# An attention and state-space kernel on one core: first loads as tasks of the list, lag 0 reordered by GpSimd, and a new order of all tasks

## The chip, the core and the metric

The kernel runs on one core of a Trainium2 chip. TensorE (PE) multiplies matrices, VectorE (DVE) and ScalarE (ACT) do elementwise work, GpSimd (POOL) copies, fills and starts transfers, and SyncE (SP) starts transfers. The metric is the device time of one execution in microseconds (us).

## The reference

Two branches read the same x (2048 positions, 640 channels) and are mixed by a gate per position. Branch a is attention over 8 positions at distances 0, 2, ... 14, with 32 heads of 20 channels. Branch b is a long convolution of x with a kernel K that is generated from 192 complex states per channel.

```
g = sigmoid((x * gate_w).sum(-1, keepdims=True))
qkv = x @ wqkv                                   # 640 -> 3 * 640
logits = q . k at 8 dilated positions, masked, * 20**-0.5
a = (softmax(logits) . v) @ wo
dt = exp(log_dt)
P = exp(dt * (A_re + i A_im) * l)                # 640 x 192 x 2048
K = Re(sum over n of C * P * dt * B)             # 640 x 2048
y = irfft(rfft(u padded) * rfft(K padded))[:L] + u * Dskip
out = g * a + (1 - g) * y
```

## The kernel before, in words

The whole program is a list of 1384 tasks (`SEQ`, L50). A number names a task, a letter behind it the engine that runs it where there is a choice: A ScalarE, D VectorE, S SyncE's queue, G GpSimd's queue. `Plan.emit` (L132) writes the tasks in that order and chains the instructions of each engine, so each engine runs its tasks strictly in the order of the list, and a task that waits holds up all that stand behind it on that engine.

The work has these parts.

- **Parameters** (`SSMParams.build`, L530). Six tiles of 128x960 (real and imaginary parts of A, B, C) become twelve bfloat16 pieces (`pc`) by some 60 instructions of VectorE and ScalarE on 128x960 float32. The pieces are stored to the DRAM tensor `Sprm`, from which kernel generation loads them. The letters in the trace: `wr`, `wi`, `tau`, `ax`, `ay`, `at`, `xl`, `xa`, `t`, `s` are tiles of this arithmetic, `dtb` is exp(log_dt).
- **Transposition of x** (`turn`, L185, ten tasks). x lies in `uga` with positions on partitions, TensorE turns it by multiplication with the identity, and ScalarE or VectorE evict 128x1024 to `bufA`.
- **Projections** (`late`, L279, sixty tasks of five matmuls) and their evictions, then attention in eight tiles of 256 positions: products of queries and keys on VectorE (`prod`, L337), sums by TensorE (`lg`, L343), maximum, exponential, normalisation, weighted values (`pv`, L406), output projection (`wo`, L430) and store to `gaS`.
- **Kernel generation** (`KGen`). Ten chunks of eight channels per quarter. For each chunk, pieces come from `Sprm` into `L` (L738), TensorE forms the arguments (`arg`, L763), ScalarE takes sines and exponentials (L775, L777, two function tables), VectorE multiplies (L794 to L796), TensorE sums over the states into `kps` (L812), and VectorE moves the sums into `E` (`fin`, L876).
- **Spectrum of the kernel** (`KSpec`). After chunk 6 and after chunk 10 the state `E` is turned (L893) and evicted to `KE` (`kev`), and for 16 blocks of constants `W`, loaded from DRAM through three buffers, TensorE forms the spectrum (`ks`, L923). In every second block it also adds lag 0, which is dt * sum(C * B) + Dskip per channel: a matmul of a row of ones with the row `KD` on a single partition (L927).
- **Convolution** (`Conv`). Rows of x come again from DRAM, are transformed (`fu`, L1038; `fp`, L1073), multiplied with the spectrum on VectorE (L1100 to L1106), transformed back (`inv`, L1131; `yp`, L1173), mixed with the attention's result and stored.

The first loads are not in the list: they are issued while the program is set up, in a fixed order. SyncE gets two parameter tiles, then all four quarters of x; ScalarE three parameter tiles and, behind three small instructions, the sixth; GpSimd the identity, three vectors, the five blocks of projection weights (held back by four copies out of the parameter tiles, L562), masks, fills and constants. Lag 0 goes through TensorE: `kdb` (128 partitions by 5) is transposed, evicted as `kdr`, stored to `kdS`, and loaded as `KD` in the order block, half, channel (L860), so that the matmul at L927 reads for each channel four values that lie 160 elements apart:

```
self.KD = kk.tile([1, 4, 2, 80], BF16, name="KD")
nc.tensor.matmul(kp[...], self.one[:], self.KD[:, :, c, 8 * c0:8 * c1].rearrange("p g x -> p x g"), ...)
```

Of the kernel before, what the change touches and what calls it, by code (L numbers as in the profile page):

```python
# [54 lines left out]
147A 187 188A 272 273 144 51 48 247 57 70 72 75 148 127G 231G 248 523 524 803 808 813 145A 274 276 275 277 227 278 160 170 228 279 229 161D 304 174 280 171A 306 175D 525
527 172 176 526 528 529 531 530 532 173D 177D 281 533 535 534 537 536 538 539 540 541 542 282 305 307 543 545 544 546 249 252 250 251D 547 549 548 550 168 169D 551 164
553 552 554 165A 134 555 557 178 556 558 559 560 569 267G 191G 521G 255 561 135D 308 310 230S 570 1128S 283 284 616 179D 563 562 571 572 573 574 575 576 256 577 309 579
253 254D 578 580 257A 581 583 311 582 584 564 565 585 213 586 587 588 312 589 313 590 591 593 592 594 566 411S 615 214D 285 567 595 597 596 598 258 599 601 259A 600 602
166 603 605 167A 604 606 221 222A 617 619 260 618 621 620 622 607 568 314 609 608 261D 612 288 623 625 624 610 627 611 626 628 629 631 630 632 262 633 635 264 263D 265D
340 342 634 636 637 639 638 640 315 641 215 643 286 216D 287D 180 642 644 645 522G 316 613 662 661 266 647 162 646 648 163A 649 317 651 217 650 652 663 665 664 666 218A  # L60
653 318 291 614 655 289 667 669 654 341 343 668 670 671 292 673 290A 344 293D 346 672 674 219 675 294 295D 658 677 656 657 676 678 679 680 220A 296 681 345 683 298 319
320 303G 707 708 682 684 685 687 686 688 659 297D 348 321 324 660 689 690 347 691 692 349 693 695 694 696 697 698 709 710 299A 300 301D 711 713 712 714 322 715 717 192
# [35 lines left out]
class Plan:  # L98
# [1239 lines left out]
```

## Time and profile before

| what | value |
|---|---|
| time, median of 3 runs (lowest, highest) | 418.91 us (416.09, 418.92) |
| profiled execution, its own time | 417.38 us |
| its span, first to last instruction | 415.5 us |
| TensorE matmul busy | 348.9 us (84%), 6687 instructions |
| VectorE busy | 308.0 us (74%), 433 instructions |
| ScalarE busy | 291.9 us (70%), 442 instructions |
| GpSimd busy | 52.3 us (13%), 94 instructions |
| moved by DMA | 49.86 MB, mean 120 GB/s |

A line of the profile groups instructions by source line, engine, operation and tile (result, arrow, operands). Tile names are the program's, with numbers left out. A busy time counts matmuls from start to modelled end, and matmuls overlap, so the time that TensorE needs for a group is read from the starts of successive rows.

### The profile page before, as it was taken

To read this page: it belongs to the slowest core of one execution; us is meant where nothing else is said; L and a number is where in the kernel's file an instruction comes from. 1 tells how busy PE (TensorE), PEld (TensorE's weight loads), DVE (VectorE), ACT (ScalarE), POOL (GpSimd) and SP (SyncE) were. 2 spreads that over 40 slices of the span, in tenths; PEclk is the share of its full clock that TensorE was granted. 3 is DMA by queue.
4 is the path that set the end of the run, shared out by engine and by line. 5 is a ranking of instruction groups with operands and counts; after the bars stand their busy time and mean duration, and the time that the engine had idled before them with its cause. 6 is when DMAs were issued, how large, how long until landed. Compare 5 with 4: busy or idle time off the path is not lost. (4 is left out here: it accounts for less than half of the span.)

```text
span 415.5 us, 15009 instructions
## 1 busy us (share of the span) xinstructions
PE 348.9 (84%) x6687; PEld 212.5 (51%) x6687; DVE 308.0 (74%) x433; ACT 291.9 (70%) x442; POOL 52.3 (13%) x94
## 2 busy tenths in 40 slices
PE   0068999977979998899977999999999994999860
PEld 0054464422435453455442555668887773777650
DVE  0059999956879999999982996894678766376883
ACT  1049999836969999999994788875666661254692
POOL 7901100140000000300120001000000050000023
PEclk9999999986989999999996999999999998699996
DMA  9920054595421152630397565424122299645027
GB/s 259 367 77 25 0 152 159 185 215 147 94 39 32 39 119 73 132 80 7 76 202 138 139 143 135 106 58 138 35 66 65 86 294 206 158 132 147 17 58 198
DMA packets 49072, 49.86 MB, mean 120 GB/s; under 512 B 26478, under 2 KB 40096, under 8 KB 49008
## 3 DMA queue, kind: packets, MB, share of 16 engines
q1 hardware_dynamic: 41072, 31.30, 29.5%
q0 software_dynamic: 4736, 16.29, 15.5%
q10 hardware_dynamic: 3200, 1.31, 1.3%
q8 instruction: 52, 0.85, 0.9%
q14 instruction: 12, 0.10, 0.1%
HBM read 37.00 MB, written 11.89 MB: 118 GB/s over the span
## 5 line engine op out<-in xcount | busy, mean ns | idle before, releaser
L775 ACT ACTIVATE big<-ar 128x576 bf16<-128x576 int16 x120 | 71.9, 653 | 20.2 <-PE ar L763 19.2
L279 PE MATMUL tb<-bufA 128*128 128x512 bf16 x300 | 76.0, 397 | 1.7 <-ACT bufA L459 0.9
L923 PE MATMUL tb<-KE,W 128*64 128x192 bf16 (+1 forms) x1280 | 63.0, 241 | 6.7 <-DMA W<-c_spec 6.7
L763 PE MATMUL ar<-Rarg,L 64*128 64x288 bf16 (+1 forms) x480 | 55.0, 282 | 11.2 <-DMA L<-Sprm 3.0
L923 PEld LDWEIGHTS <-W 128*64 128x64 bf16 x1280 | 47.4, 113 | 21.6 <-issue 12.3
L406 DVE TENSOR_TENSOR pv<-vc,asb 128x4096 bf16<-128x4096 bf16 (+1 forms) x24 | 46.0, 1928 | 11.2 <-DMA aS<-at 7.9
L777 ACT ACTIVATE big<-ar 128x832 bf16<-128x832 f32 x60 | 49.2, 880 | 3.0 <-PE ar L763 2.5
L279 PEld LDWEIGHTS <-bufA 128*128 128x128 bf16 x300 | 33.2, 121 | 34.1 <-issue 12.6
L763 PEld LDWEIGHTS <-L 64*128 64x128 bf16 x480 | 20.0, 94 | 49.3 <-issue 41.7
L459 ACT ACTIVATE bufA<-tb 128x384 bf16<-128x384 f32 (+1 forms) x34 | 17.6, 523 | 25.0 <-PE tb L923 15.8
L812 PE MATMUL kps<-tbx 128*32 128x20 bf16 (+1 forms) x2560 | 26.2, 175 | 4.9 <-issue 4.9
L812 PEld LDWEIGHTS <-tbx 128*32 128x32 bf16 (+1 forms) x2560 | 22.5, 91 | 11.3 <-issue 7.9
L927 PE MATMUL tb<-KD,one 1*64 1x192 bf16 (+1 forms) x128 | 27.9, 433 | 0.0
L430 PE MATMUL tb<-wo_sb,oT 128*128 128x320 bf16 x160 | 27.3, 306 | 0.0
L337 DVE TENSOR_TENSOR prod<-qk 128x2048 bf16<-128x2048 bf16 x20 | 24.0, 1218 | 1.2 <-PE lg L343 1.2
L796 DVE TENSOR_TENSOR tbx<-big 128x1280 bf16<-128x1280 bf16 x30 | 24.5, 817 | 0.0
L412 PE MATMUL tb<-pv,ind 128*64 128x512 bf16 (+1 forms) x192 | 23.0, 358 | 1.7 <-DVE pv L406 1.6
L337 DVE TENSOR_TENSOR prod<-uga 128x2048 bf16<-128x2048 bf16 x20 | 24.1, 1219 | 0.0
L459 ACT ACTIVATE big<-ar 128x1024 bf16<-128x1024 f32 x17 | 17.1, 1023 | 9.9 <-PE ar L1038 9.6
L459 ACT ACTIVATE tbx<-ar 128x512 bf16<-128x512 f32 (+1 forms) x26 | 16.9, 697 | 9.8 <-issue 4.4
L185 PE MATMUL ar<-ident,uga 128*128 128x128 bf16 x80 | 9.6, 298 | 16.6 <-DMA uga<-in_A_x_dram 12.9
L459 ACT ACTIVATE bufA<-ar 128x1024 bf16<-128x1024 f32 x9 | 9.0, 1020 | 17.4 <-PE ar L185 17.4
(178 smaller groups left out, 565.1 us busy)
## 6 DMA issues: line engine op xcount, KB each, us to landing
W<-c_spec SPq DMA_DIRECT2D x32, 320.0 KB, 3.2
vc<-vS POOLq DMA_DIRECT2D x10, 327.5 KB, 5.7
Sprm<-pc SPq DMA_DIRECT2D x12, 240.0 KB, 3.4
L<-Sprm SPq DMA_DIRECT2D x80, 36.0 KB, 2.5
uga<-in_A_x_dram SPq DMA_DIRECT2D x4, 640.0 KB, 15.6
gaS<-ga SPq DMA_DIRECT2D x8, 320.0 KB, 2.9
bufA<-in_A_wqkv_dram POOLq DMA_DIRECT2D x5, 480.0 KB, 7.0
uga<-gaS POOLq DMA_DIRECT2D x7, 320.0 KB, 11.8
```

The costliest lines, as they stand in the source:

```text
L279: nc.tensor.matmul(ppf, self.wq[:, kt, which * D + e:(which + 1) * D:5], self.xT[:, c0 // 1024, kt, c0 % 1024:c0 % 1024 + SC], start=(kt = ...
L337: nc.vector.tensor_tensor(b[e][:], self.part(ch, 0)[:, e, o:o + C].unsqueeze(1).to_broadcast([128, W, C]), win(self.part(ch, 1)[:, e, :], ...
L406: nc.vector.tensor_tensor(b["pv", e][:, 0:2 * n], taps, aw, ALU.mult)
L430: nc.tensor.matmul(apf[:, :320], b["oT"][:, e, i * 128:(i + 1) * 128], wo_sb[:, e, hf * 320:(hf + 1) * 320], start=(e == 0), stop=(e == 4))
L459: nc.scalar.activation(o, i, ACT.Identity)
L763: nc.tensor.matmul(ar[:, g2, a0:a0 + ncol], L[rows, sb, gp, l0:l0 + 128], R[rows, c0:c0 + ncol], start=True, stop=True, tile_position=(64 ...
L775: nc.scalar.activation(dst[:, 2 * gp:2 * gp + 2, sub, :], ar[:].bitcast(I16)[:, :, 0:2 * SW:2], ACT.Sin, scale=SCL)
L777: nc.scalar.activation(dst[:, 2 * gp:2 * gp + 2].rearrange("p g s n -> p g (s n)"), ar[:, :, 0:2 * EW], ACT.Exp)
L796: nc.vector.tensor_tensor(qq[:, :, :, :], trg[:, :, KI:].rearrange("p a (v m) -> p a v m", v=2), exq[:, :, KI:].unsqueeze(2).to_broadcast( ...
L812: nc.tensor.matmul(kps[32 * g:32 * g + 32, h, NM * ql:NM * ql + NM], pt[rows, k, v, :], qq[rows, k, v, :], start=(g not in started), stop= ...
L923: nc.tensor.matmul(kp[64 * c:64 * c + 64, fl], w["t"][:, nf * h + fl, m, :], self.KE[p][:, m, c].rearrange("p x g -> p (x g)"), start=(m = ...
L927: nc.tensor.matmul(kp[64 * c:64 * c + 64, fl], self.one[:], self.KD[:, :, c, 8 * c0:8 * c1].rearrange("p g x -> p x g"), start=False, stop ...
```

## The change

There are four parts.

1. **First loads as tasks.** The loads of x (4), projection weights (5), parameter tiles (6), three vectors and the small constants become tasks, with a queue chosen for each by the list (SyncE, ScalarE or GpSimd). What needs them names them as dependencies. The four delaying copies go. The parameter tiles now hold channel 5p+k on partition p, so a partition's five rows are one piece of 1,920 bytes in DRAM; `Sprm` is laid out by channel, and a store to it is 640 pieces of 384 bytes instead of 128 of 1,920. exp(log_dt) is taken straight from the loaded vector; only gate_w is still turned by TensorE.
2. **Lag 0.** TensorE's transposition of `kdb` and its eviction go. `kdb` is stored as it lies, loaded as four rows into the first partition of `E` (`KR`), and one GpSimd copy writes `KD` in the order half, channel, block. The matmul then reads `KD` in adjacent columns. The first `fin`, which writes `E`, waits for that copy.
3. **Kernel state.** The four evictions of the turned state (`kev`) keep their sizes; they write pairs of neighbouring elements, block by block of PSUM in alternation, where they wrote one block's elements and then the other's, each eight bytes apart.
4. **A new order of all tasks** (1411 of them), with some evictions moved between ScalarE and VectorE.

```diff
 SEQ = """
-1130S 92 1119G 93A 82 83A 84 85D 0 1 4 94 88 89A 95A 80 78 79A 15 81A 3 9 11 2 12A 8 6 13D 10 14 76 77A ...
+13S 12S 24 18A 16S 23 35 36A 37A 20G 14S 15S 0G 4G 21 32 25 28 29 39 3S 22D 38 41 27 26 30 10S 8G 9S ...
...
-        xl = [lambda sc=sc: nc.sync.dma_start(self.xn[sc // 2][...], xr[:, 4 * sc:4 * sc + 4]) for sc in range(4)]
-        wl = [lambda kt=kt: nc.gpsimd.dma_start(self.wq[:, kt], wr[:, kt]) for kt in range(NKT)]
+        self.xl = [pl.add(f"ldx{sc}", "SAG", lambda e, sc=sc: queue(nc, e).dma_start(self.xn[sc // 2][...], xr[:, 4 * sc:4 * sc + 4])) for sc in range(4)]
+        self.wl = [pl.add(f"ldw{kt}", "SAG", lambda e, kt=kt: queue(nc, e).dma_start(self.wq[:, kt], wr[:, kt])) for kt in range(NKT)]
...
-            m = pl.add(f"turn{n}", "P", turn, acq=["ar"])
+            m = pl.add(f"turn{n}", "P", turn, deps=[self.lid] + self.xl[2 * hf:2 * hf + 2], acq=["ar"])
...
-        self.S = dr.tile([128, NPC, 5, NST], BF16, name="Sprm")
+        self.S = dr.tile([D, NPC, NST], BF16, name="Sprm")
...
-            eng.dma_start(t[nm][:], ap.rearrange("(k p) n -> p k n", p=128))
+            ld[nm] = pl.add(f"ld{nm}", "SA", lambda e, nm=nm, ap=ap: queue(nc, e).dma_start(t[nm][:], ap.rearrange("(p k) n -> p k n", k=5)))
...
-        nc.tensor.matmul(lt[:, 0, 0:15], lg10[:], ident[0:15, 0:15], start=True, stop=True)
-        nc.scalar.activation(dtb[:], lt[:, 0, 0:5], ACT.Exp)
-        for n, nm in enumerate(("cre", "bre", "cim", "bim")):
-            nc.gpsimd.tensor_copy(at.wq[:, 0, 2 * n:2 * n + 2], t[nm][:, 0, 0:2])
+        ld["dt"] = pl.add("dtx", "A", lambda _: nc.scalar.activation(dtb[:], ldt[:, 0], ACT.Exp), deps=[ld[0]], table="exp")
...
-            op(f"sp{i}", "S", lambda _: nc.sync.dma_start(self.S[:, i], t[k][:]), [k], [f"S{i}"])
+            op(f"sp{i}", "S", lambda _: nc.sync.dma_start(self.S.rearrange("(p k) i n -> i p k n", k=5)[i], t[k][:]), [k], [f"S{i}"])
...
-        self.KD = kk.tile([1, 4, 2, 80], BF16, name="KD")
+        self.KR = self.E[0:1].rearrange("o m c -> o (m c)")[:, 0:640].rearrange("o (g x) -> o g x", g=4)
+        self.KD = kk.tile([1, 2, 80, 4], BF16, name="KD")
...
-            nc.tensor.matmul(b["kd"][0:5, 0, 0:128], prm.kdb[:], ident[:], start=True, stop=True)
-            queue(nc, e).dma_start(self.kdS.rearrange("(k p) -> k p", p=128), self.kdr[:])
+            queue(nc, e).dma_start(self.kdS.rearrange("(p k) -> p k", k=5), prm.kdb[:])
+            queue(nc, e).dma_start(self.KR.rearrange("o (a b) x -> o a b x", a=2), self.kdS.rearrange("(o b a x) -> o a b x", o=1, b=2, a=2))
+        self.kd = pl.add("kdp", "G", lambda _: nc.gpsimd.tensor_copy(self.KD[:].rearrange("o c x g -> o (c x) g"), self.KR.rearrange("o g x -> o x g")), deps=[t])
...
-        return pl.add(f"fin{c}", "D", fn, deps=[m] + (self.moved if c == c0 and p else []), ...)
+        return pl.add(f"fin{c}", "D", fn, deps=[m] + ([self.kd] if c == 0 else self.moved if c == c0 else []), ...)
...
-                evict(nc, en, self.KE[p][:].rearrange("p m c x g -> p g (m c x)")[:, 2 * t:2 * t + 2], b["nx"][:, :, 0:2 * M5 * n])
+                evict(nc, en, self.KE[p][:].rearrange("p m c x g -> p (m c x) g")[:, :, 2 * t:2 * t + 2], b["nx"][:, :, 0:2 * M5 * n].rearrange("p g x -> p x g"))
...
-                                nc.tensor.matmul(kp[...], self.one[:], self.KD[:, :, c, 8 * c0:8 * c1].rearrange("p g x -> p x g"), ...)
+                                nc.tensor.matmul(kp[...], self.one[:], self.KD[:, c, 8 * c0:8 * c1].rearrange("p x g -> p (x g)"), ...)
```

The order of VectorE's first instructions, before (`bufA<-ar` is an eviction of turned x):

```order
L174 MEMSET zz 128x35
L461 CAST bufA<-ar 128x1024
L583 TENSOR_TENSOR wr<-cre,bre 128x960
L583 TENSOR_TENSOR t_142<-cim,bim 128x960
L583 TENSOR_TENSOR wr<-wr,t_142 128x960
L583 TENSOR_TENSOR t_143<-cim,bre 128x960
L631 TENSOR_REDUCE k_121<-wr 128x5
```

and with the change:

```order
L173 MEMSET zz 128x35
L574 TENSOR_TENSOR wr<-cre,bre 128x960
L574 TENSOR_TENSOR tau<-aim,dtb 128x960
L621 TENSOR_TENSOR dt_111<-dtb 128x5
L574 TENSOR_TENSOR t_114<-cim,bim 128x960
L574 TENSOR_TENSOR wr<-wr,t_114 128x960
L459 CAST gw_sb<-ar 128x5
L577 SCALAR_TENSOR_TENSOR tau<-tau,s_125 128x960
L574 TENSOR_TENSOR t_115<-cim,bre 128x960
L574 TENSOR_TENSOR wi<-cre,bim 128x960
```

The eviction of x stood ahead of all parameter arithmetic; now the arithmetic stands first, and the first eviction of x comes as the thirteenth instruction behind the fills. The six products of queries and keys (L337, now L335) that stood among the parameter arithmetic stand behind it, but for one.

SyncE's queue at the start of the program, before (`uga` takes x, `L` here takes constants of the convolution):

```order
L539 DMA cre<-in_B_C_re_dram 128x5x192
L539 DMA cim<-in_B_C_im_dram 128x5x192
L166 DMA uga<-in_A_x_dram 128x4x640 x4
L1018 DMA L<-c_phi 128x1536
L611 DMA Sprm<-pc 128x960 x2
```

and with the change:

```order
L538 DMA bre<-in_B_B_re_dram 128x960
L538 DMA cre<-in_B_C_re_dram 128x960
L538 DMA aim<-in_B_A_im_dram 128x960
L538 DMA cim<-in_B_C_im_dram 128x960
L538 DMA bim<-in_B_B_im_dram 128x960
L166 DMA uga<-in_A_x_dram 128x4x640
L167 DMA bufA<-in_A_wqkv_dram 128x1920 x4
L538 DMA are<-in_B_A_re_dram 128x960
L166 DMA uga<-in_A_x_dram 128x4x640
```

Five of the six parameter tiles now stand ahead of x on this queue, two quarters of x went to GpSimd's, and four of the five weight blocks came from it.

GpSimd's queue around lag 0, before:

```order
L305 DMA vS<-pv 640x1x512
L331 DMA vc<-vS 64x10x262 x4
L305 DMA vS<-uga 640x1x512
L856 DMA kdS<-kdr 5x128
L300 COPY uga<-qk 128x14 x5
L860 DMA KD<-kdS 1x4x160
```

and with the change:

```order
L303 DMA vS<-pv 640x1x512
L847 DMA kdS<-kdb 128x5
L851 DMA E<-kdS 1x4x160
L855 COPY KD<-E 1x640
L303 DMA vS<-uga 640x1x512
```

The store, the load and the new copy stand together, and the two loads of values (`vc`) that stood ahead of them have gone to SyncE's queue.

## Rows read from the trace of the kernel before

**Rows 1.** Busy time by stretch: PE, PEld, DVE, ACT, POOL, clock, DMA share, GB/s.

```profile
90.00:100.00 10.00, 7.68 (x40) 2.41 (x38) 5.99 (x6) 6.49 (x10) 0.58 (x1) 0.67 0.88 230
...
90.00:200.00 110.00, 100.00 (x2201) 49.86 (x2199) 96.03 (x125) 99.13 (x153) 5.54 (x11) 0.94 0.35 80
200.00:230.00 30.00, 24.57 (x396) 11.44 (x398) 20.15 (x25) 22.81 (x32) 4.68 (x6) 0.89 0.77 144
230.00:340.00 110.00, 109.64 (x2306) 76.53 (x2306) 84.89 (x120) 79.27 (x125) 6.12 (x11) 1.00 0.42 113
340.00:360.00 20.00, 13.26 (x256) 9.82 (x250) 8.79 (x17) 4.35 (x7) 3.14 (x5) 0.74 0.95 207
360.00:390.00 30.00, 30.00 (x730) 22.24 (x728) 20.97 (x46) 13.74 (x20) 0.00 (x0) 1.00 0.40 113
```

**Rows 2.** Timeline of the start: start, duration, work, idle before and its releaser.

```profile
4.50 0.18 POOL L562 COPY bufA<-cre 128x2 bf16<-128x2 bf16 x1 [0.47 <-DMA cre<-in_B_C_re_dram]
...
20.36 0.61 PE L185 MATMUL ar<-ident,uga 128*128 128x128 bf16 x4 [11.70 <-DMA uga<-in_A_x_dram]
...
22.80 1.94 ACT L459 ACTIVATE bufA<-ar 128x1024 bf16<-128x1024 f32 x2 [13.79 <-PE ar L185]
...
24.92 1.23 DVE L461 CAST bufA<-ar 128x1024 bf16<-128x1024 f32 x1 [23.89 <-PE ar L185]
```

**Rows 3.** Timeline, end of the parameters: VectorE's last subtraction, first L loads.

```profile
77.56 1.16 DVE L613 TENSOR_TENSOR s<-at,pc 128x960 f32<-128x960 f32 x1
...
83.45 3.70 SPq L738 DMA_DIRECT2D L<-Sprm  x8
```

**Rows 4.** Groups by shape: line, count, busy us, mean ns, idle before.

```profile
L279 PE MATMUL tb<-bufA 128*128 128x512 bf16 x300 | 76.0, 397 | 1.7 <-ACT bufA L459 0.9 <-ACT uga L459 0.9
...
L337 DVE TENSOR_TENSOR prod<-uga 128x2048 bf16<-128x2048 bf16 x20 | 24.1, 1219 | 0.0
...
L1038 PEld LDWEIGHTS <-uga 128*64 128x64 bf16 x320 | 19.7, 204 | 1.5 <-issue 1.4
...
L459 ACT ACTIVATE bufA<-tb 128x384 bf16<-128x384 f32 x29 | 14.6, 511 | 9.1 <-PE tb L927 7.3 <-PE tb L923 1.8
...
L775 ACT ACT_TABLE_LOAD x6 | 7.7, 1283 | 3.2 <-issue 3.2
...
L927 PEld LDWEIGHTS <-one 1*64 1x64 bf16 x128 | 6.8, 102 | 7.9 <-issue 0.7
```

**Rows 5.** Instructions of tile KE, the evictions: shortest, median, longest in ns.

```profile
L459 ACT ACTIVATE KE<-ar x4: 1627/1995/2336, 208.5 to 335.5; 128x960 bf16<-128x960 f32 x2, 128x640 bf16<-128x640 f32 x2
```

**Rows 6.** Timeline of TensorE, spectrum matmuls and lag 0, both parts.

```profile
287.53 0.60 PE L923 MATMUL tb<-KE,W 128*64 128x192 bf16 x10
288.06 0.49 PE L927 MATMUL tb<-KD,one 1*64 1x192 bf16 x2
288.48 0.60 PE L923 MATMUL tb<-KE,W 128*64 128x192 bf16 x10
...
380.69 0.38 PE L927 MATMUL tb<-KD,one 1*64 1x128 bf16 x2
381.00 0.47 PE L923 MATMUL tb<-KE,W 128*64 128x128 bf16 x10
```

**Rows 7.** Timeline of TensorE, two projections at either clock level.

```profile
82.53 2.35 PE L279 MATMUL tb<-bufA 128*128 128x512 bf16 x10
...
89.84 4.04 PE L279 MATMUL tb<-bufA 128*128 128x512 bf16 x10
```

**Rows 8.** DMA issues: queue, count, KB each, median us to landing.

```profile
Sprm<-pc SPq DMA_DIRECT2D x12, 240.0 KB, 3.4
...
kdS<-kdr POOLq DMA_DIRECT2D x1, 1.2 KB, 10.4
KD<-kdS POOLq DMA_DIRECT2D x1, 1.2 KB, 2.8
```

**Rows 9.** Timeline of VectorE, the first chunk's sums into E.

```profile
125.53 0.48 DVE L876 CAST E<-kps 128x320 bf16<-128x320 f32 x1
```

More of the change, by code (lines that the diff above doesn't have):

```diff
@@ L109, in add, with ops @@
         return t
-    def ops(self, ops):
-        wrote, read = {}, {}
+    def ops(self, ops, wrote):
+        wrote, read = dict(wrote), {}
         for name, eng, fn, rd, wr, more in ops:
@@ L155, in __init__, with loads @@
         self.aS = dr.tile([2, 32, W, 256], BF16, name="aS")
-    def loads(self, bufA, uga, cst):
+    def loads(self, pl, bufA, uga, cst):
         nc = self.nc
@@ L235, in plan_gate, with consts @@
         return m, v
-    def consts(self, cst, keep):
+    def consts(self, pl, cst, keep):
         nc = self.nc
@@ L331, in values @@
                     queue(nc, e).dma_start(t[64 * w:64 * w + 64], self.vS.rearrange("(p a) e s -> p (a e) s", a=2)[:, :, c0 + HV * DIL * w:c0 + HV * DIL * w + NV])
-            vc = pl.add(f"vc{c0}", "SG", values, deps=[self.stored[k] for k in range(ch + 1)], acq=["vc"])
+            vc = pl.add(f"vc{c0}", "SG", values, deps=[self.zst] + [self.stored[k] for k in range(ch + 1)], acq=["vc"])
             lgs = []
@@ L680, in build @@
             step()
-        wrote = pl.ops(ops)
+        wrote = pl.ops(ops, ld)
         self.kdb, self.kd = kdb, wrote["kd"]
@@ L702, in __init__ @@
                 nc.gpsimd.memset(L[64 * g2:64 * g2 + 2], 1.0)
-            self.Lb.append(L)
-        self.R = cst.tile([128, SW + EW], BF16, name="Rarg")
-        nc.gpsimd.dma_start(self.R[:], nc.inline_tensor(_arg_consts(), name="c_rarg").ap())
+        self.blank = [pl.add(f"lset{i}", "G", lambda _, L=L: blank(_, L)) for i, L in enumerate(self.Lb)]
+        self.lr = pl.add("ldr", "SAG", lambda e: queue(nc, e).dma_start(self.R[:], r_d))
     def open(self, big, tbx):
@@ L836, in __init__ @@
         self.w_d = self.nc.inline_tensor(_spec_consts(), name="c_spec").ap()
-        self.kdr = keep.tile([5, 128], BF16, name="kdr")
         self.one = keep.tile([1, 64], BF16, name="one")
@@ L876, in fn @@
             nc.vector.tensor_copy(e[:, :, :, CQ * cl:CQ * cl + CQ], b["kps"][:, :, 0:CQ * NM].rearrange("p c (q m) -> p c m q", m=NM))
-        return pl.add(f"fin{c}", "D", fn, deps=[m] + (self.moved if c == c0 and p else []), after=fins[-1:], rel=[("kb", m0)])
+        return pl.add(f"fin{c}", "D", fn, deps=[m] + ([self.kd] if c == 0 else self.moved if c == c0 else []), after=fins[-1:], rel=[("kb", m0)])
     def part(self, pl, p, f, pa, ps, ident, sk, opened, free):
@@ L1224, in gated_mix_kernel @@
     acst = c2.enter_context(tc.tile_pool(name="a2_cst", bufs=1))
-    more = at.consts(acst, keep)
-    xl, wl = at.loads(cv.bufA, cv.uga, acst)
-    params = prm.build(c1, tc, pl, B_A_re, B_A_im, B_B_re, B_B_im, B_C_re, B_C_im, B_log_dt, B_Dskip, gate_w, at, keep, pa, xl, wl)
-    more()
-    kg = KGen(keep, cv.pool, tc, prm)
+    at.consts(pl, acst, keep)
+    at.loads(pl, cv.bufA, cv.uga, acst)
+    params = prm.build(c1, tc, pl, B_A_re, B_A_im, B_B_re, B_B_im, B_C_re, B_C_im, B_log_dt, B_Dskip, gate_w, at, keep, pa)
+    kg = KGen(pl, keep, cv.pool, tc, prm)
     at.aq = c2.enter_context(tc.tile_pool(name="a2_q", bufs=2))
```

175 lines of the change are left out of this document (83 added, 92 removed).

## The prediction

> **What bounds the kernel now.** I read the busy time by stretch first, then the first microseconds in order of time, then single lines by shape. In the stretches the reader is to see that two kinds of time are open. From 90 to 200 us all of TensorE, VectorE and ScalarE are busy nearly throughout (100.0, 96.0 and 99.1 of 110 us); from 230 to 340 us TensorE has 109.6 of 110 us and the two others under 85; from 360 to 390 us TensorE has all 30 [rows 1]. So behind 90 us work leaves the time only if it leaves the full engine, TensorE above all. The other open time is the start: the first parameter tile is there at 4.50 us, when GpSimd's copy stops waiting for it, but TensorE's first transposition of x waits until 20.36 us, ScalarE's first eviction until 22.80 us and VectorE's first computing instruction until 24.92 us, because that is an eviction of such a transposition and the parameter arithmetic stands behind it in the queue [rows 2]. From there to the last parameter subtraction at 77.56 us VectorE runs nearly without a gap, and the first load of kernel parameters (L) goes out at 83.45 us [rows 3]. All ten chunks of kernel generation wait for that load.
>
> **The head.** The new list puts eleven instructions of the parameter chain ahead of VectorE's first eviction of x and sends the six parameter tiles first. VectorE can start at about 5 us [rows 2]. Before, the way from its first instruction to the end of the last subtraction is 77.56 + 1.16 - 24.92 = 53.8 us [rows 2, 3]. Ahead of that subtraction six products of queries and keys fall away, 6 x 1.22 = 7.3 us [rows 4], and one reduction over 128x960, about 1.2 us by the subtraction of that size [rows 3]; of the small things that go (first tile's maximum and normalisation) and come (two evictions of x) I take 0.5 us: 9 us in all. New waits come at the front: the second product needs the third tile and the exponential of log_dt, the wrap needs two ScalarE results, three products need the fourth and fifth tile. I allow 5 us, between 2 and 11. So the subtraction ends at 5 + 53.8 - 9 + 5 = 55 us, and with the 4.7 us that follow now (83.45 - 78.72, [rows 3]) the first L load goes out at 59.5 us, **24 us earlier**.
>
> That is not all gain. What was taken out is done later, in stretches that are full: 9 us on VectorE; on TensorE 34 projections stood ahead of the last parameter store and now 22, 12 x 1.18 us = 14 us by the unthrottled row [rows 7]; on ScalarE the list now needs 19 table loads for 16, 3 x 1.28 = 3.9 us [rows 4]. The charge lies between 9 (VectorE alone, the others beside it) and 18 us (TensorE and the tables in series). I take 11, near the lower end, since the engines do this work beside each other. **Net: -13 us**, bounds -19 (24 + 4 for fewer waits, less 9) and 0 (24 - 6 for more waits, less 18).
>
> **Lag 0.** The row of ones with KD is 128 matmuls, 64 pairs. In the first part a pair starts 0.42 us before what follows it (288.06 to 288.48), while five ordinary pairs of the same 192 columns take 0.53 us (287.53 to 288.06), 0.11 each; in the second part, of 128 columns, the pair takes 0.31 us (380.69 to 381.00) [rows 6]. KD was read four columns at a time, each from a place 320 bytes on; after the change its columns lie side by side. If this order is the price, a pair saves 0.42 - 0.11 = 0.31 us in the first part and 0.31 - 0.08 = 0.23 us in the second (0.08 for 128 columns is my estimate, 0.11 scaled by 128/192). 32 x 0.31 + 32 x 0.23 = 17.3 us. [...] If the price belongs to the single row, nothing is saved. I take the order: a weight load of 64 columns from places 320 bytes apart (F1's, out of uga) takes 204 ns, a load of 64 adjacent columns from the single row of ones 102 ns [rows 4]; the stride doubles a read there and the single row does not. [...]
>
> All of this is TensorE time in stretches where TensorE is the full engine [rows 1]. VectorE and ScalarE have 25 us of room in 230 to 340 us, so I count nine tenths: **-15 us**, bounds -18 and -11.
>
> On GpSimd the values now go out as they lie, come back, and are reordered by one copy; the TensorE transposition and its eviction disappear, under 0.5 us. The first fin, on VectorE, now waits for that copy. Store and load took 10.4 and 2.8 us to land [rows 8]; with the copy at 1 to 4 us (no row shows its form) it is some 18 us behind the start of the store, which stands near the first L load. The first fin comes 125.53 - 83.45 = 42 us behind that load [rows 3, 9]. Some 24 us of cover: cost 0. If the copy were later than the fin, VectorE's products behind it and the next chunk's sums would wait.
>
> **Eviction of the kernel state.** Four ScalarE instructions of 1.63 to 2.34 us [rows 5]. They now write pairs of neighbours and read PSUM in alternation from two banks. The nearest row is the eviction of the spectrum, which also reads PSUM in steps and writes pairs: 384 columns in 0.51 us [rows 4], so 960 would take some 1.3 us and 640 some 0.85. Saving 2 x 1.0 + 2 x 0.8 = 3.6 us on ScalarE, half of it on the path to the first spectrum matmuls: **-2 us**. [...] Bounds -3.6 and +2.
>
> **Parameter layout.** Loads are 128 pieces of 1,920 bytes for 640 of 384, stores to Sprm the other way round. A store lands in 3.4 us now [rows 8]; only the last one is on the path, and even twice that costs 3 us, inside the head's bounds. GpSimd's four delaying copies and the three small ScalarE instructions at the start lie in idle time: 0.
>
> **The two stalls.** 200 to 230 us and 340 to 360 us have TensorE at 24.6 of 30 and 13.3 of 20 us, with the DMA engines at 0.77 and 0.95 [rows 1]: rows of x, later psi and the attention's rows, come in one burst. In the new list these bursts stand together again, but one load of values no longer stands behind the first. **-1 us**, bounds -8 and +8.
>
> **Sum.** -13 - 15 - 2 - 1 = -31 us on the profiled execution's 417.38 us: 386.4 us. The median of the runs is 1.5 us above that execution, so 388 us. The bounds, taken as independent, give 14 us to either side: 374 to 402.
>
> **Rivals.** (1) *The price of lag 0 is the single row.* For it: no row shows a single row with adjacent columns as the moving side. Against: the 102 ns above. 388 + 15 = 403 us. Chance 0.07. (2) *The head's gain is given back.* The deferred 12 projections and 9 us of VectorE work end up in series in a stretch that is full already [rows 1]: 388 + 13 = 401 us. For it: three engines above nine tenths from 90 to 200 us. Against: there TensorE's busy time counts matmuls that overlap, 397 ns each in the table [rows 4] but 0.24 apart (ten in 2.35 us, [rows 7]). Chance 0.07. (3) *TensorE falls to its low level in kernel generation.* [...] Chance 0.04. (4) *The change does not do what it says*: x, the projection weights and the parameters share the same DMA engines and arrive no earlier, and the KD read stays slow: 418 us, chance 0.04.
>
> **The numbers.** My forecast has 0.78. Predicted 388 us. The range reaches from 372 to 404 us, to take in rivals 1 and 2 and a little below my lower bound; it leaves out rivals 3 and 4 and a tenth at the edges. About 1% is what this kernel's measurement can tell (its three runs lie 0.7% apart). Faster by over 1%: 0.78 + 0.07 + 0.07 = 0.92; within 1%: 0.04; slower: 0.04.
>
> **What would show it.** In the profile after: VectorE's first product near 5 us and the first L load at 55 to 65 us; a KD pair at about 0.1 us to the next start; KE evictions near 1.3 us; the first fin not waiting for GpSimd; the last chunk's fin some 15 to 25 us earlier than now. I am wrong on the head if the first L load is early but the fifth chunk's fin is not; wrong on lag 0 if the KD pairs keep 0.3 to 0.4 us; wrong on the stalls if TensorE waits for W or L longer than now.

## The result and the profile after

The changed kernel takes **400.52 us** (median of 4 runs, 399.45 to 401.80) beside 418.92 us for the kernel before (4 runs, 416.09 to 420.37): a ratio of **0.957, 95% interval 0.951 to 0.963**. On another chip, later, it took 401.37 us beside 417.60 us, 0.9645 (0.960 to 0.969). A ratio leaves out the executions that ran over 1.5% above the fastest of their kernel, while a median takes in all, so a ratio can differ a little from the quotient of the medians. The prediction of 388 us had the direction and most of the mechanism and was 12 us too low. The profiled execution took 401.13 us, its span is 399.3 us: 16.2 us less than before, where the sum said 31.

The busy times by stretch, columns as in [rows 1]:

```profile
90.00:200.00 110.00, 100.39 (x2042) 49.82 (x2056) 95.44 (x122) 99.25 (x156) 11.25 (x19) 0.98 0.31 69
200.00:230.00 30.00, 23.15 (x518) 12.88 (x518) 18.49 (x21) 19.53 (x35) 1.43 (x2) 0.83 1.02 169
230.00:340.00 110.00, 102.29 (x2285) 77.09 (x2284) 79.80 (x121) 77.02 (x116) 7.92 (x13) 0.97 0.46 124
340.00:360.00 20.00, 17.91 (x406) 14.74 (x404) 8.83 (x21) 10.97 (x18) 0.00 (x0) 0.81 0.59 141
360.00:390.00 30.00, 24.19 (x786) 20.41 (x784) 23.75 (x45) 21.62 (x36) 3.38 (x6) 1.00 0.26 72
```

Kernel generation up to 200 us is as full as it was and runs at a granted clock of 0.98. The hole at 200 to 230 us is wider than before: TensorE has 23.15 of 30 us where it had 24.57, the DMA share went from 0.77 to 1.02 and the clock from 0.89 to 0.83.

The head and GpSimd's part of lag 0 (timeline: start, duration, work, idle before and its releaser), answering [rows 2, 3, 9]:

```profile
4.28 1.16 DVE L574 TENSOR_TENSOR wr<-cre,bre 128x960 f32<-128x960 bf16 x1 [3.24 <-DMA cre<-in_B_C_re_dram]
...
52.41 1.16 DVE L604 TENSOR_TENSOR s<-at,pc 128x960 f32<-128x960 f32 x1
...
57.71 3.74 SPq L733 DMA_DIRECT2D L<-Sprm  x8
...
73.76 1.99 POOL L855 COPY KD<-E 1x640 bf16<-1x640 bf16 x1 [2.72 <-DMA E<-kdS]
...
102.83 0.48 DVE L865 CAST E<-kps 128x320 bf16<-128x320 f32 x1
```

VectorE's first product starts at 4.28 us, the last subtraction at 52.41 us and the first L load at 57.71 us, 25.7 us earlier. GpSimd's copy is done at 75.8 us, 27 us ahead of the first sums into `E`, which do not wait.

Lag 0 on TensorE, answering [rows 6]:

```profile
219.60 0.60 PE L912 MATMUL tb<-KE,W 128*64 128x192 bf16 x10
220.13 0.27 PE L916 MATMUL tb<-KD,one 1*64 1x192 bf16 x2
220.33 0.60 PE L912 MATMUL tb<-KE,W 128*64 128x192 bf16 x10
...
330.34 0.24 PE L916 MATMUL tb<-KD,one 1*64 1x128 bf16 x2
330.51 0.47 PE L912 MATMUL tb<-KE,W 128*64 128x128 bf16 x10
330.92 0.24 PE L916 MATMUL tb<-KD,one 1*64 1x128 bf16 x2
```

From start to start the pair now takes 0.20 us (220.13 to 220.33) for 0.42, and in the second part 0.17 for 0.31. Five ordinary pairs take 0.53 us, and in the second part 0.41, so 0.11 and 0.08 each: the pair keeps 0.09 us more than an ordinary one.

The evictions of the kernel state, answering [rows 5] (shortest, median, longest in ns):

```profile
L457 ACT ACTIVATE KE<-ar x4: 689/877/1065, 193.6 to 308.4; 128x960 bf16<-128x960 f32 x2, 128x640 bf16<-128x640 f32 x2
```

**Where the 16 us come from.** The starts of the same piece of work in both spans, in us. Chunks are counted from 0 here and below, so chunk 5 is the sixth, the last of the first part:

| mark | before | after | earlier by | change since the mark above |
|---|---|---|---|---|
| first L load | 83.5 | 57.7 | 25.7 | -25.7 |
| sums of chunk 5 into E | 202.2 | 188.7 | 13.5 | +12.2 |
| first spectrum matmul | 220.1 | 219.6 | 0.5 | +13.0 |
| second part's first spectrum matmul | 338.8 | 324.9 | 13.9 | -13.4 |
| end of the span | 415.5 | 399.3 | 16.2 | -2.3 |

Up to chunk 5 the head seems to behave as foreseen. Then all of it seems lost within one stretch, and as much comes back in the next. The busy times of these two stretches (same columns) help to tell what is only moved there and what is lost. Before:

```profile
202.20:220.10 17.90, 14.04 (x308) 7.28 (x304) 13.75 (x21) 16.24 (x21) 4.68 (x6) 0.99 0.88 160
220.10:338.80 118.70, 116.77 (x2345) 78.99 (x2345) 88.79 (x121) 82.44 (x130) 4.92 (x9) 0.97 0.42 110
```

After:

```profile
188.70:219.60 30.90, 23.82 (x366) 11.12 (x367) 23.12 (x28) 20.14 (x33) 3.77 (x5) 0.83 0.92 158
219.60:324.90 105.30, 103.22 (x2318) 75.91 (x2316) 78.82 (x116) 81.22 (x125) 2.70 (x5) 1.00 0.41 114
```

The list puts more work ahead of the first spectrum matmul: chunk 6's sums came 14.0 us behind it (234.1) and now come 4.6 us behind it (224.2). Where that work comes from is told by TensorE's weight loads (PEld), one for each matmul, counted by line in each stretch. (Of the changed kernel's projections 22 matmul records of 300 are missing in the trace, but no weight load.)

| work | ahead of the first spectrum matmul: before, after | behind it: before, after |
|---|---|---|
| projections | 15, 25 | 0, 0 |
| weighted values (L412, now L410) | 8, 32 | 96, 80 |
| output projection | 15, 20 | 85, 80 |
| arguments of chunks | 32, 48 | 112, 100 |
| sums of products (L343, now L341) | 16, 24 | 40, 36 |

Of the 63 more ahead of the mark, 37 are missing behind it: they are only moved. The other 26 stood ahead of chunk 5's sums before. They are work that the new list defers, past chunk 5 even. At the rates at full clock (0.24 us for a matmul of a projection [rows 7]; by the starts in the changed kernel's timeline from 188.7 to 201 us, at a granted clock of 1.00, 0.13 for one of weighted values and 0.07 to 0.15 for the others) each of the two groups takes some 4 us. So of the 13.0 us some 4 are moved work, some 4 are deferred work, and **some 5 us are lost**. Two things make up the loss. TensorE's idle time in the stretch grew from 17.9 - 14.0 = 3.9 to 30.9 - 23.8 = 7.1 us, and part of its work ran at the low clock:

```profile
191.50 1.05 PE L410 MATMUL tb<-pv,ind 128*64 128x512 bf16 x8
...
200.40 12.56 SPq L993 DMA_DIRECT2D uga<-in_A_x_dram  x5
...
203.68 1.66 PE L807 MATMUL kps<-tbx 128*32 128x20 bf16 x179
211.82 0.26 PE L807 MATMUL kps<-tbx 64*32 64x20 bf16 x13 [6.48 <-issue]
...
214.41 1.92 PE L410 MATMUL tb<-pv,ind 128*64 128x512 bf16 x8
```

This is the after kernel's timeline again. Five of the eight loads of x's rows go out on SyncE at 200.40 us and hold its queue for 12.56 us (three more go on GpSimd's). In the middle of chunk 6's 192 matmuls of line 807 TensorE stands still for 6.48 us, and no tile, semaphore or DMA of the program releases it: "issue". Behind it the same eight matmuls take 1.92 us that took 1.05 before it. The granted clock was 0.50 from 212.0 to 217.8 us:

```profile
212.00:217.80 5.80, 5.80 (x41) 1.95 (x31) 1.43 (x2) 4.05 (x8) 0.00 (x0) 0.50 1.24 199
```

That is 5.8 x (1 - 1.05 / 1.92) = 2.6 us; with up to 3.2 us more idle time it makes the 5 us, as closely as this working can tell.

The low clock is not new, however. In the kernel before it came as well, but just behind the mark (stretch, then timeline):

```profile
219.60:226.50 6.90, 6.90 (x63) 2.82 (x62) 0.70 (x1) 2.77 (x6) 0.00 (x0) 0.51 0.84 149
...
220.13 1.01 PE L923 MATMUL tb<-KE,W 128*64 128x192 bf16 x10
221.08 0.51 PE L927 MATMUL tb<-KD,one 1*64 1x192 bf16 x2
221.52 1.01 PE L923 MATMUL tb<-KE,W 128*64 128x192 bf16 x10
```

Five ordinary pairs take 0.95 us from start to start there, for 0.53 at full clock, so some 3 us of the 6.9 were lost, and they count into the stretch behind the mark. That stretch is 13.4 us shorter now: 32 x 0.22 = 7.0 us by lag 0 (the run b_lag0c below, with lag 0 alone, shortens it from 118.7 to 111.7 us), some 4 by the moved work, and the remaining 2.4 in the main by this low clock, which has gone from it. So the first burst costs some 5 - 2.4 = **2.6 us more than before**. The two stretches together say the same: they take 136.2 us, 6.6 more than the 136.6 - 7.0 us that lag 0 should leave, and of these 6.6 us some 4 are deferred work and 2.6 the burst. The sum is read from the marks; its parting in two is an estimate by counts and rates.

In the last stretch lag 0 saves TensorE 32 x 0.14 = 4.5 us and only 2.3 show. That is not the new list's doing: in b_lag0c, which has the old one, the same stretch falls from 76.7 to 74.7 us, by 2.0.

The second burst is that of the attention's rows, later:

```profile
325.44 5.22 POOL L1142 DMA_DIRECT2D uga<-gaS  x8 [12.96 <-PE ar L1027]
...
331.09 1.08 PE L1062 MATMUL ar<-big,L 128*64 128x128 bf16 x32
337.81 2.34 PE L912 MATMUL tb<-KE,W 128*64 128x128 bf16 x40 [5.64 <-DMA W<-c_spec]
```

Eight loads of 320 KB leave GpSimd within 5.2 us, and TensorE, which is through with its transforms, waits 5.64 us for a W on SyncE's queue. TensorE's waits in total (us, times, longest) show both bursts; before:

```profile
PE tb L923 <- DMA W<-c_spec: 6.7, 3, 4.5
PE kps L812 <- issue: 4.9, 3, 3.0
```

after:

```profile
PE kps L807 <- issue: 9.7, 4, 6.5
PE tb L912 <- DMA W<-c_spec: 8.6, 4, 5.6
```

### The profile page after: what moved, and what is told of

Read it like the earlier page. It is cut to its first block, busy times and chain, and to the rows that moved or that the text cites. A ratio compares the mean times of both kernels' runs of the same rounds, so it can differ in the third digit from the quotient of the medians.

```text
span 399.3 us, 14980 instructions
## 1 busy us (share of the span) xinstructions
PE 333.3 (83%) x6664; PEld 209.5 (52%) x6686; DVE 300.0 (75%) x420; ACT 302.3 (76%) x456; POOL 50.9 (13%) x82
## 5 line engine op out<-in xcount | busy, mean ns | idle before, releaser
L758 PEld LDWEIGHTS <-L 64*128 64x128 bf16 x480 | 19.0, 95 | 52.3 <-issue 48.8
L457 ACT ACTIVATE bufA<-tb 128x384 bf16<-128x384 f32 (+1 forms) x36 | 18.9, 528 | 20.6 <-PE tb L912 11.7
L457 ACT ACTIVATE tbx<-ar 128x512 bf16<-128x512 f32 (+1 forms) x31 | 20.4, 699 | 11.6 <-PE ar L1062 7.5
L1089 DVE TENSOR_TENSOR tbx<-tbx,bufA 128x768 bf16<-128x768 bf16 (+1 forms) x32 | 14.5, 487 | 19.1 <-ACT bufA L457 14.0
L335 DVE TENSOR_TENSOR prod<-qk 128x2048 bf16<-128x2048 bf16 x20 | 24.1, 1220 | 4.1 <-PE lg L341 2.2
L335 DVE TENSOR_TENSOR prod<-uga 128x2048 bf16<-128x2048 bf16 x20 | 24.1, 1220 | 3.3 <-PE lg L341 3.1
L457 ACT ACTIVATE big<-ar 128x1024 bf16<-128x1024 f32 x19 | 18.7, 1023 | 7.3 <-PE ar L1027 7.1
L410 PE MATMUL tb<-pv,ind 128*64 128x512 bf16 (+1 forms) x192 | 23.1, 365 | 0.0
L789 DVE TENSOR_TENSOR tbx<-big 128x1024 bf16<-128x1024 bf16 x30 | 20.5, 685 | 1.0 <-ACT big L770 0.5
L790 DVE TENSOR_TENSOR tbx<-big 128x1024 bf16<-128x1024 bf16 x30 | 20.5, 685 | 0.0
```

The lines of the kernel that those rows point to most:

```text
L335: nc.vector.tensor_tensor(b[e][:], self.part(ch, 0)[:, e, o:o + C].unsqueeze(1).to_broadcast([128, W, C]), win(self.part(ch, 1)[:, e, :], ...
L410: nc.tensor.matmul(b["op", e][64 * a:64 * a + 64, 0:n, :], self.twin, b["pv", e][:, a:2 * n:2, w, :], start=(w == 0), stop=(w == HV - 1), ...
L457: nc.scalar.activation(o, i, ACT.Identity)
L758: nc.tensor.matmul(ar[:, g2, a0:a0 + ncol], L[rows, sb, gp, l0:l0 + 128], R[rows, c0:c0 + ncol], start=True, stop=True, tile_position=(64 ...
```

## The experiments

All were timed beside the kernel before, in three batches of which each had one chip. "ks" below is the first spectrum matmul.

### Lag 0

**Alone in the kernel before** (b_lag0). This one's load of the four rows is issued after the first sums into `E` and overwrites 640 elements of E's first partition, so the sums that lie there are lost; the work is the same.

```diff
-        self.KD = kk.tile([1, 4, 2, 80], BF16, name="KD")
+        self.KR = self.E[0:1]...[:, 0:640].rearrange("o (g x) -> o g x", g=4)
+        self.KD = kk.tile([1, 2, 80, 4], BF16, name="KD")
...
-        queue(nc, e).dma_start(self.KD[:]..., self.kdS...)
+        queue(nc, e).dma_start(self.KR..., self.kdS...)
+        nc.gpsimd.tensor_copy(self.KD[:].rearrange("o c x g -> o (c x) g"), self.KR.rearrange("o g x -> o x g"))
...
-        self.KD[:, :, c, 8 * c0:8 * c1].rearrange("p g x -> p x g")
+        self.KD[:, c, 8 * c0:8 * c1].rearrange("p x g -> p (x g)")
```

> The kernel before with the lag-0 part alone: KD is loaded as four rows into the first partition of E and written by one GpSimd copy in the order half, channel, block; TensorE's transposition of kdb stays. Theory (the order of the columns is the price, TensorE is the full engine): a KD pair falls from 0.42 and 0.31 us to the 0.20 and 0.17 us that the changed kernel shows, 32 x 0.22 + 32 x 0.14 = 11.5 us of TensorE time, so 407 to 411 us. Rival (VectorE and ScalarE are nearly as full, the time is given back as waits): the pairs are as short, but the time falls by less than 5 us, 414 to 418 us.

Measured: 0.9796 (0.973 to 0.986) of the time before, 8.5 us. GpSimd's queue, in its timeline, shows the price of the late place:

```profile
124.82 0.58 POOL L861 DMA_DIRECT2D E<-kdS  x1 [37.47 <-DVE E L878]
```

GpSimd stands 37.47 us until the first sums have left `E`; nobody waited for GpSimd long enough to undo the gain. The next run places the load earlier.

**The same with the load placed ahead of the first sums** (b_lag0c): the load and the copy are one task, moved up in the list by its place alone.

> The kernel before with the change of lag 0 alone, the load of the four rows and GpSimd's copy now standing in the list ahead of the first fin, where E's first partition is still free. If the order of the columns is the price of lag 0 and TensorE is the full engine in both stretches: the 64 pairs save the 11.3 us that the pair rows of the changed kernel show, nine tenths of it to the end: 408 to 410 us. If the gain is given back in the two stalls (TensorE's time is not the limit there): 414 to 418 us. If undoing lag 0 in the changed kernel cost 8 us only because of the new list: under 4 us here.

Measured: 409.13 us (6 runs) beside 417.60, **0.978 (0.972 to 0.984)**, 8.5 us. Its timeline on GpSimd and TensorE:

```profile
98.64 1.24 POOL L862 COPY KD<-E 1x640 bf16<-1x640 bf16 x1 [1.93 <-DMA E<-kdS]
...
286.08 0.27 PE L929 MATMUL tb<-KD,one 1*64 1x192 bf16 x2
286.27 0.60 PE L925 MATMUL tb<-KE,W 128*64 128x192 bf16 x10
```

The pair is at 0.19 us without any other part of the change, and 8.5 of the 11.5 us that the pairs save reach the end. The first theory's 408 to 410 us hold. The stretch between the two parts' first spectrum matmuls, to be compared with 118.70 us before, shows the whole saving of the first part:

```profile
221.60:333.30 111.70, 109.70 (x2345) 78.75 (x2345) 87.72 (x120) 82.28 (x130) 4.90 (x9) 0.98 0.44 112
```

From there to the end it takes 408.0 - 333.3 = 74.7 us, 2.0 less than before, where the pairs save 4.5.

**Undone in the changed kernel** (a_kdslow): `KD` again in the order block, half, channel, the copy and the matmul's reading to fit, all else as changed.

```diff
-        self.KD = kk.tile([1, 2, 80, 4], BF16, name="KD")
+        self.KD = kk.tile([1, 4, 2, 80], BF16, name="KD")
...
-        nc.gpsimd.tensor_copy(self.KD[:].rearrange("o c x g -> o (c x) g"), self.KR.rearrange("o g x -> o x g"))
+        nc.gpsimd.tensor_copy(self.KD[:].rearrange("o g c x -> o g (c x)"), self.KR)
...
-        self.KD[:, c, 8 * c0:8 * c1].rearrange("p x g -> p (x g)")
+        self.KD[:, :, c, 8 * c0:8 * c1].rearrange("p g x -> p x g")
```

> The changed kernel with KD written by GpSimd in the old order, so that TensorE reads columns 320 bytes apart again; all else as changed. Theory (order of the columns is the price): KD pairs back at 0.42 and 0.31 us, 410 to 413 us. Rival (the single row is the price, or the time is covered): 400 to 403 us.

Measured: 408.77 us, 0.9773 (0.972 to 0.982): by the ratios 5 to 8.5 us above the changed kernel and a little under the forecast. The pair is back at its old price, with the same one row and the same ones:

```profile
223.34 0.49 PE L916 MATMUL tb<-KD,one 1*64 1x192 bf16 x2
223.76 0.60 PE L912 MATMUL tb<-KE,W 128*64 128x192 bf16 x10
```

0.42 us from start to start. The order of the columns alone makes 0.22 of 0.42 us; rival 1, that the single row is the price, falls.

### The kernel state's eviction alone (b_kev)

```diff
-                evict(nc, en, self.KE[p][:].rearrange("p m c x g -> p g (m c x)")[:, 2 * t:2 * t + 2], b["nx"][:, :, 0:2 * M5 * n])
+                evict(nc, en, self.KE[p][:].rearrange("p m c x g -> p (m c x) g")[:, :, 2 * t:2 * t + 2], b["nx"][:, :, 0:2 * M5 * n].rearrange("p g x -> p x g"))
```

> The kernel before with the kernel-state eviction alone in the new order of columns. Theory: the four evictions fall from 2.34 and 1.64 us to about 1.05 and 0.75 us, 4.4 us of ScalarE time, and the time by 1 to 3 us, 416 to 418 us. Rival (they stand beside a stall that ends last anyway): no change, 418 to 420 us.

Measured: 418.97 us, 1.0001 (0.996 to 1.004). The four instructions are down to 0.70 to 0.99 us in its trace, and none of it is seen at the end: the interval leaves room for 1.7 us either way.

### The head

**The order alone** (b_first): the kernel before, with 18 tasks of the parameter chain put at the front of its list; loads and all else unchanged.

```diff
-1130S 92 1119G 93A 82 83A 84 85D 0 1 4 94 ...
+1130S 1119G 0 1 4 3 2 6 8 15 5 16 7 11 12A 13D 14 17 28 20 92 93A ...
```

> The kernel before with 18 parameter tasks (VectorE and ScalarE) moved to the front of the list, ahead of the evictions of x; loads and all else as before. Theory (VectorE's idle 24 us at the start is worth about 13 us in the end, unless a later stall takes it): the first L load 8 to 14 us earlier than 83.5 us, the fifth chunk's fin and the last chunk's fin 6 to 12 us earlier, 407 to 413 us. Rival (the head is given back at the burst of x rows, as the changed kernel's fin of chunk 5 at 188.7 and first spectrum at 219.6 us suggest): fin of chunk 5 earlier by as much, but the first spectrum matmul within 3 us of 220 and the time 415 to 419 us.

Measured: 415.61 us (10 runs), 0.9947 (0.992 to 0.998). VectorE does start early, in its timeline

```profile
4.84 1.16 DVE L583 TENSOR_TENSOR wr<-cre,bre 128x960 f32<-128x960 bf16 x1 [3.81 <-DMA bre<-in_B_B_re_dram]
...
39.61 0.69 DVE L461 CAST uga<-tb 128x512 bf16<-128x512 f32 x1 [8.89 <-PE tb L279]
```

but the first L load goes out at 80.6 us, only 2.9 us earlier, and chunk 5's sums only 2.1 us (200.0). The time, 2.2 us less by the ratio, lies in the rival's range, but not for the rival's reason: there is no head start that the burst could take. VectorE loses 8.89 us of its start in one place, where the eviction of a projection stands in its queue and TensorE has not made that projection yet. The early first instruction was worth 2.9 us of the L load here, while work of the same engine that waits for something else still stood in the rest of the chain.

**The changed kernel with late parameters** (a_params_late): two of the four loads of x and four of the five weight blocks stand ahead of the parameter tiles in the list, nothing else moves.

> The changed kernel with two quarters of x and four of the five weight blocks put ahead of the parameter tiles on SyncE's queue; all else as changed. It takes the early parameters away. Theory (the head's gain comes from VectorE starting on parameters at once): first product at 11 to 14 us instead of about 5, the first L load 6 to 9 us later than 57.7 us, the fifth chunk's fin later by 4 to 9 us, 402 to 409 us. Rival (what is won at the head is lost at the burst of x rows): L and fins later, but the first spectrum matmul still at 218 to 222 us and 399 to 402 us.

Measured: 415.66 us (10 runs), 0.9916 (0.987 to 0.997), by the ratios 11 to 14.5 us above the changed kernel and above both forecasts. VectorE's first product starts at 19.26 us and the first L load goes out at 69.6 us, 11.9 us later. TensorE pays for it at once (wait: total, times, longest):

```profile
PE ar L184 <- DVE gw_sb L459: 13.1, 1, 13.1
```

VectorE's eviction for the first transposition stands behind the parameter products in its queue, so a late parameter holds TensorE too. The loss at the end is about that of the first L load; how much of it is VectorE's late start and how much TensorE's, this run does not separate.

### The two bursts

**Rows of x spread** (a_rows): the eight loads all on SyncE, each behind another of SyncE's transfers instead of side by side. **The attention's rows spread** (a_gaf): those eight on SyncE, one behind every first or second W. **Both** (a_rows_gaf).

```diff
-... 1147S 1148S 1149S 1150G 1151G 1152S 1153S 1154G 402 421 ...
+... 1147S 421 424 ... 1049 1148S 456 1149S 845 1150S ... 438 1151S 850 855 1152S 860 1153S ... 511S 1154S ...
...
-... 1360G ... 1361G 1362G 1363G 1364G 1365G 1366G ... 1367G ...
+... 1107 1360S 1110 1113 1361S ... 1119 1362S 1122 1125 1363S ... 1128 1364S ... 1131 1365S ... 1137 1366S ... 1143 1367S ...
```

> The changed kernel with the eight loads of rows of x spread over SyncE's queue between other tasks, from the store of attention tile 3 to the load of values of tile 7, instead of standing together on two queues. Theory (the stall of TensorE from 205.3 to 211.8 us, put down to issue, is its instruction fetch behind these loads, and 5 of them block SyncE's queue for 12.6 us): the stall goes, the first spectrum matmul comes at 205 to 212 us instead of 219.6, the time falls by 5 to 12 us to 388 to 396 us. Rival (TensorE would wait there for VectorE's products or the attention's loads anyway): first spectrum matmul at 217 to 221 us, 399 to 402 us.

> The changed kernel with the eight loads of the attention's result moved from GpSimd's queue, where they go out together at 325 us, to SyncE's queue, one behind each second load of W. Theory (the W loads wait behind them: TensorE waits 5.6 and 1.9 us for W and its clock is at 0.70 and 0.67 from 330 to 350 us): those waits go, 390 to 395 us. Rival (W has three buffers and is late anyway, or SyncE's queue now delays W): 399 to 403 us.

> Both loads spread as in the two kernels that do one each. If the two stalls are separate, the gains add: 380 to 388 us. If one only hides the other, the better of the two singles.

Measured, in this order: 397.33 us, 0.9488 (0.944 to 0.954); 398.14 us, 0.9497 (0.941 to 0.959); 392.28 us, 0.9362 (0.930 to 0.942). Each single run lies between its theory and its rival, and the third misses the 380 to 388 us. By the ratios, against the changed kernel's two (0.957 and 0.9645), the gains are 3.4 to 6.6, 3.1 to 6.2 and 8.7 to 11.8 us, so the two about add. In the first, ks comes at 213.8 us for 219.6 and the whole gain stays to the end of the span (393.3 for 399.3). In the second the longest wait for a W falls from 5.6 to 1.4 us. The traces give the wait of the first theory as issue; that it is an instruction fetch is the author's guess.

**Again, on one chip with the changed kernel** (after_again, a_rows_gaf_again), and **the same 16 loads on SyncE, but at the places where the change has them** (a_sp_together):

```diff
-... 1147S 1148S 1149S 1150G 1151G 1152S 1153S 1154G ...
+... 1147S 1148S 1149S 1150S 1151S 1152S 1153S 1154S ...
...
-... 1360G ... 1361G 1362G 1363G 1364G 1365G 1366G ... 1367G ...
+... 1360S ... 1361S 1362S 1363S 1364S 1365S 1366S ... 1367S ...
```

> The changed kernel as it is, on the same chip as the other runs of this batch, so that they can be compared with it directly: 400.5 us, 0.957 of the kernel before.

> The changed kernel with the rows of x and the attention's rows spread among SyncE's other transfers, a second time, beside the changed kernel itself. If the bursts cost what TensorE's waits show (6.5 us at one instruction fetch, 5.6 at one W): 392 us, 8 us below the changed kernel. If the first time was chance: 396 to 400 us.

> The changed kernel with the same 16 loads at their places in the list, all on SyncE's queue and none on GpSimd's. If it is the burst that costs (many large transfers at once): no gain, 398 to 403 us, and TensorE still waits 5 us or more at one instruction of kernel generation behind the rows of x. If it is the queue (GpSimd's transfers collide with SyncE's): as the spread version, 392 to 395 us. If the attention's rows on SyncE hold back the W loads behind them: 403 to 412 us.

Measured (6 runs each):

| kernel | median, us | ratio to before | 95% interval |
|---|---|---|---|
| after_again | 401.37 | 0.9645 | 0.960 to 0.969 |
| a_sp_together | 393.65 | 0.9401 | 0.934 to 0.946 |
| a_rows_gaf_again | **390.77** | **0.9348** | 0.929 to 0.940 |

The spread version is the best of all, 10.6 us below the changed kernel beside it. Its first stretch, busy times as above, and TensorE's timeline there:

```profile
190.60:215.00 24.40, 22.01 (x371) 10.85 (x367) 22.23 (x28) 19.98 (x34) 0.86 (x2) 1.00 0.42 95
```

```profile
205.73 1.66 PE L807 MATMUL kps<-tbx 128*32 128x20 bf16 x179
209.40 0.24 PE L807 MATMUL kps<-tbx 64*32 64x20 bf16 x13 [2.01 <-issue]
```

The stretch from chunk 5's sums to ks is 24.4 us for 30.9, at full clock and with 2.4 us of idle time for 7.1. TensorE is busy 22.01 us in it, 8.0 more than the 14.04 us before the change: the moved and the deferred work, as counted above.

I had expected that a_sp_together would decide between burst and queue by its time, and the number it hit, 392 to 395 us, was the queue's. The trace says otherwise. SyncE's queue and TensorE in its timeline:

```profile
203.28 12.80 SPq L993 DMA_DIRECT2D uga<-in_A_x_dram  x8
...
213.69 0.26 PE L807 MATMUL kps<-tbx 64*32 64x20 bf16 x13 [4.84 <-issue]
...
309.28 22.56 SPq L900 DMA_DIRECT2D W<-c_spec  x8
331.89 0.43 SPq L1142 DMA_DIRECT2D uga<-gaS  x1
333.82 16.33 SPq L900 DMA_DIRECT2D W<-c_spec  x8
```

The first burst is still one, and TensorE still waits 4.84 us at the same instruction. The second is none any more. On SyncE the attention's rows stand behind loads of W that each wait for a free buffer, and only one of the eight goes out before 350 us. TensorE is busy 10.00 of 10.00 us at 330 to 340 us here, 4.36 in the changed kernel, and this trace has no wait for a W among TensorE's ten longest. So for the second burst it is enough that the loads do not go out on GpSimd's queue, on which all eight went within 5.2 us (325.44 in the changed kernel); the first needs the spreading itself, for the stretch from chunk 5's sums to ks is still 29.3 us here. By their times alone this kernel and the spread one are not told apart: their intervals overlap.

## Why the prediction was right, and where not

The forecast had the direction right, and the time lies in its range, near the upper end. But all four terms gave less than was forecast, in the same direction: the head by some 3.5 us, lag 0 by 5.7, the eviction by 2, the stalls by 3.6.

**Head: -13 us predicted, some -9.5.** The first L load was put at 59.5 us and is at 57.7. The deferred work was put at 11 us; the stretch from there to chunk 5 grew by 12.2 us, and some 4 us more come behind that mark, 16 in all, inside the bounds of 9 and 18. That chunk 5's sums come 13.5 us earlier is thus agreement at one mark: chunk 2's come 33.9 us earlier (158.6 to 124.7), the last chunk's only 5.1 (300.5 to 295.4) where 15 to 25 were to show. A single mark also moves with the order of the list. And b_first shows that VectorE's early start alone, with which the working of this step began, is worth 2.9 us of the L load; the rest of the 25.7 us needs other work out of the chain's way as well.

**Lag 0: -15 us predicted, some -9.3.** The mechanism was right (a_kdslow), and the step that was mis-sized has two parts. The pairs save 32 x 0.22 + 32 x 0.14 = 11.5 us, not 17.3: I took an ordinary pair as the new price, 0.11 us, but the pair keeps 0.09 us above it in both parts. The bound of -11 us counts a rest of only 0.06 us a pair, 13.5 us in all; no run shows that term, and with the 0.09 us that the trace shows it was too high. What the 0.09 us are, no run says. And nine tenths were to reach the end. In the first part all 7.0 us do; in the second 2.3 of 4.5 (2.0 in b_lag0c). There the first 17.6 us (338.8 to 356.4), in which TensorE waits for W, stay as long as they were in b_lag0c (17.7 us, 333.3 to 351.0). With 9.3 us the term lies outside its bounds of 11 and 18.

**Eviction: -2 us predicted, 0 by b_kev.** The size was right, even cautious (1.04 and 1.06 us where I put 1.3). The claim that half of it lies on the path was wrong. Reading the two banks in alternation, and writing pairs instead of single elements eight bytes apart, the eviction of 960 columns needs less than half of the 2.34 us it took. Reading and writing changed together, so no run says what either does alone. For the bound of +2 us no run shows a cause; what b_kev leaves open is 1.7 us either way.

**The cover for GpSimd: 0 predicted, 0.** The copy took 1.99 us (1.24 in b_lag0c) and ended 27 us ahead of its reader; 24 had been worked out.

**Stalls: -1 us predicted, some +2.6.** This step had the sign wrong. The text said that the bursts "stand together again" and that one load of values fewer would stand behind the first. The first costs some 2.6 us more than before. At the second, the waits for W went from 6.7 to 8.6 us, which was the sign given for being wrong here, but the end shows no more loss than b_lag0c with the old list.

**The sum.** By what was measured it is -9.5 - 9.3 + 2.6 = -16.2 us, the difference of the spans; it must come out so, since it is made of the marks, and only the parting of 6.6 us between head and burst is an estimate. The working of the range has a slip: taken as independent, the terms' bounds give 10 us below and 17 above, not 14 to either side. With the bursts spread, 26.8 us are gained, near the 31 predicted. That is luck, for these 10.6 us more come from the stalls, which the forecast took to stay nearly as they were. What spreading would be worth in the kernel before was not tried.

**The rivals.** Rival 1 fell (a_kdslow). Rival 2 gave 401 us, the time that was measured, but only a part of its mechanism is seen: some 3.5 of the 13 us of the head are given back, as deferred work that came to 16 us for 11. Rival 3 fell (granted clock 0.98 from 90 to 200 us, for 0.94 before), and so did rival 4.

## What to carry to other kernels

The head start shrank here at the next hole, from 25.7 us at the first L load to 0.5 at the first spectrum matmul: follow the same piece of work by its start through both traces, and where the lead shrinks, count matmuls on both sides of the mark to tell moved and deferred work from lost time. Then look whether the kernel before lost the same time behind the mark. The list sends its bulk loads side by side, and behind them TensorE stood still for 6.48 us in the first burst and waited 5.64 us for one W in the second; one load behind every first or second load that waits for a buffer anyway cost TensorE no wait for a W over 1.4 us. And the one row read as a moving operand took 0.42 us a pair with its columns 320 bytes apart and 0.20 us with adjacent columns, so that a copy of 1.99 us on an idle engine paid.

## What the runs showed of the hardware

TensorE's longest pause with no releaser was longer when the program's data were on their way. In line 807's small matmuls every version of the changed kernel has such pauses, the longest of 2.0 to 7.0 us. With the DMA engines otherwise idle (a_rows_gaf_again, 207 to 211 us; queue: packets, MB, share of 16 engines) only the queue for instructions moves anything,

```profile
q8 instruction: 2, 0.03, 2.9%
```

and the pause, from 207.4 to 209.4 us, is 2.01 us; the two packets lie at 207.0 and 210.5 us, outside it. In the changed kernel the same pause falls into the burst (208 to 212 us; the packets' times overlap, hence the share over 100%):

```profile
q1 hardware_dynamic: 2178, 0.69, 130.9%
...
q8 instruction: 1, 0.02, 2.2%
```

and lasts 6.48 us, at the same instruction, the 180th of chunk 6's 192. With all eight loads on SyncE (a_sp_together) it was 4.84 us. What the pause is, no run shows. That TensorE fetches its next instructions in it is the author's guess, here and in the expectations; the trace does not tie a packet of that queue to an engine's wait.

A single-row moving operand whose columns lie 320 bytes apart took 0.42 us a pair of 192 columns (the kernel before and a_kdslow), one with adjacent columns 0.20 us (the changed kernel). The slow read did not follow TensorE's clock: where the granted clock was 0.51 (219.6 to 226.5 us in the kernel before), the pair took 0.44 us (221.08 to 221.52), while five ordinary pairs went from 0.53 to 0.95 us.
